# Sixteen instead of six weight chunks decoded during the first attention batch, later ones in three steps

## The chip, the cores and the metric

The kernel runs on one core of a Trainium2 chip. The metric is the device time of one execution in microseconds (us). The kernel before took 1181.28 to 1185.04 us in three runs, median 1183.97. One more execution was recorded by the profiler; everything read from a trace here comes from it.

## The reference

Attention with a threshold, then two feed-forward networks (FFN), one behind the other. The shapes are batch 4, 8 heads, 576 positions, head size 64; the FFNs see 2304 tokens of width 512 and have 2048 hidden units.

```python
scores = matmul(q, k.T) / sqrt(64)
scores = where(scores >= max(scores) - tau, scores, -1e9)
attn = softmax(scores)                       # over the last axis
x = matmul(attn, v)                          # heads side by side: 2304 x 512
h = x @ moe_w_in                             # first FFN: leaky, alpha per hidden unit
x = (max(h, 0) + alpha * min(h, 0)) @ moe_w_out
h = x @ moe2_w_in                            # second FFN
out = (h * clip(h + 3, 0, 6) / 6) @ moe2_w_out
```

Activations are float32, but the four weight matrices arrive as float64.

## The kernel before

**Attention** goes over 16 pairs of heads, 4 pairs for each of the 4 batches, and each pair has 9 tiles of queries: 144 tiles, 36 to a batch. A tile (`do_S`, `soft`) is a score matmul into PSUM, a row maximum and a threshold on VectorE, an exponential on ScalarE, and a masked sum on VectorE. Every second tile is followed by a division on GpSimd, transposes, and the product with v. Loads, splits and transposes for the next pair (`prep`) are emitted between the tiles of the present one.

**The FFNs** go over blocks of 512 tokens, one for each batch, and a block of the 256 left-over tokens. Each block passes through layer 1 and layer 2 with 16 hidden slices (`ft`). `h_group` makes one slice: 12 matmuls with the chunk `wi` of the input weights, an activation and a split of the result. `o_group` multiplies four slices with their chunks `wo` of the output weights. A list of such groups (`queue`) is worked off beside the attention of the following batches: block 0 runs beside the attention of batch 1, and so on. The last batch's block and the left-overs come behind the attention.

**Weights.** Each of the four matrices has 16 chunks, 64 in all, and is used once for each block. A value is used as two float32r parts, high and low: `split` copies the high part on ScalarE and subtracts it for the low part on VectorE or GpSimd (L102, L103). For its first use a chunk must also be decoded from float64 to float32. `decode_load` fetches 512 KB into one of three raw buffers (`raw64`). `decode` runs two instructions on ScalarE (L149, L150), three on VectorE (L151, L153, L154) and one on GpSimd (L155), and stores the 256 KB result to a scratch in device memory (L157). Its result `f` lies in the `stage` pool, which has four slots and also takes the loads from scratch (`st`, L170). Later blocks load the chunk from scratch and split it.

The first six chunks are decoded between the tiles of the first batch (`decode_early`, `EARLY = 6`); they are loaded back from scratch when block 0 comes to them. The other 58 are fetched by `fetch` and decoded and split by `ready`, both called from `h_group` of block 0, one group ahead of the use. The split parts lie in the pools `wip` (two chunks of `wi`) and `wop` (five chunks of `wo`).

**The order** on each engine is not that of the code. A scheduler takes the instructions of all engines by priority as soon as it expects their inputs and slots to be there; attention has its priority raised (`tc.high_priority`). On the chip each engine then works through its list in that fixed order, and all DMAs here are issued by SyncE (SP), in one list too.

Of the kernel before, what the change touches and what calls it, by code (L numbers as in the profile page):

```python
# [27 lines left out]
def f32(ap):  # L28
    return ap.bitcast(F32)
# [3 lines left out]
def kernel(  # L33
# [17 lines left out]
    NF = DFF // P  # L51
# [7 lines left out]
    NB = S // P  # L59
    W = S + SR  # L60

    EARLY = 6
    LAG = 3

    OG = 4
# [11 lines left out]
    def pool(stack, name, bufs, **kw):  # L77
        return stack.enter_context(tc.tile_pool(name=name, bufs=bufs, **kw))

    const = pool(ctx, "const", 1)  # L80
    stage = pool(ctx, "stage", 4)
    gp = pool(ctx, "gp", 5)
    tmp = pool(ctx, "tmp", 2)
    wip = pool(ctx, "wip", 2)
# [16 lines left out]
    def split(hi, lo, src, lo_eng):  # L101
        nc.scalar.copy(hi, src)  # L102
        lo_eng.tensor_tensor(out=lo, in0=src, in1=f32(hi), op=ALU.subtract)  # L103
# [3 lines left out]
    wide = moe_w_in.dtype != F32  # L107
# [7 lines left out]
    def chunk(nm, ft):  # L115
        w = weights[nm]
        if nm[0] == "i":
            n = w.shape[1] // NF
            return w[:, ft * n:(ft + 1) * n].rearrange("(k p) f -> p k f", p=P)
        return w[ft * P:(ft + 1) * P, :]  # L120
# [2 lines left out]

    RA, RB, RG = 27, 19, 20
    raw64 = []
    for i in range(3 if wide else 0):
        t = const.tile([P, RA * RB, 2], U32, name=f"raw64{i}")
        nc.gpsimd.memset(t[:, DM:], 0)
        raw64.append(t)

    def rows(ap):
        return ap.rearrange("p (a b) -> p a b", a=RA)[:, :, 0:RB]

    def st_tile(dt, name):
        return stage.tile([P, RA * RB], dt, tag="st", name=name)

    def decode_load(nm, ft):
        raw = raw64.pop(0)
        raw64.append(raw)
        dst = raw[:, 0:DM]  # L140
        dst = dst.rearrange("p (k f) a -> p k (f a)", k=NKT) if nm[0] == "i" else dst.rearrange("p n a -> p (n a)")
        nc.sync.dma_start(dst, chunk(nm, ft))
        return raw

    def decode(nm, ft, raw):
        f = st_tile(U32, "f")
        cl = dec.tile([P, RA * RG], U32, tag="cl", name="cl", bufs=2)
        low = dec.tile([P, RA * RG, 2], U16, tag="low", name="low", bufs=2)
        nc.scalar.activation(rows(low[:, :, 0]), rows(raw[:, :, 0]), AF.Copy, scale=2.0 ** -29)  # L149
        nc.scalar.activation(f32(f), f32(raw[:, :, 1]), AF.Abs)  # L150
        nc.vector.tensor_scalar(out=rows(low[:, :, 1]), in0=rows(raw.bitcast(U16)[:, :, 3]), scalar1=0x8000, scalar2=0x4000,  # L151
                                op0=ALU.bitwise_and, op1=ALU.bitwise_xor)
        nc.vector.tensor_scalar(out=rows(f32(cl)), in0=rows(f32(f)), scalar1=F64_HI, scalar2=F64_LO, op0=ALU.min, op1=ALU.max)  # L153
        nc.vector.tensor_single_scalar(rows(f), rows(cl), 3, op=ALU.logical_shift_left)  # L154
        nc.gpsimd.tensor_tensor(out=rows(f), in0=rows(f), in1=rows(low.bitcast(U32).rearrange("p n a -> p (n a)")), op=ALU.add)  # L155
        f = f32(f)[:, 0:DM]
        nc.sync.dma_start(scratch[nm, ft], f)  # L157
        return f

    raws = {}  # L160

    def w_fetch(key, nm, ft, fresh=False):
        if key in raws:
            return
        if wide and fresh:
            raws[key] = decode_load(nm, ft)
            return
        t = st_tile(F32, "st")[:, 0:DM]
        if wide:
            nc.sync.dma_start(t, scratch[nm, ft])  # L170
        elif nm[0] == "i":
            nc.sync.dma_start(t.rearrange("p (k f) -> p k f", k=NKT), chunk(nm, ft))
        else:
            nc.sync.dma_start(t, chunk(nm, ft))
        raws[key] = t
# [3 lines left out]
    passes = [(layer, b) for b in list(range(B - 1)) + [None] for layer in (1, 2)]  # L179
    decoded = set()  # L180
    ws = {}

    def w_of(kind, c):
        layer, blk = passes[c // NF]
        nm, ft = f"{kind}{layer}", c % NF
        return nm, ft, layer, blk, blk == 0 and (nm, ft) not in decoded

    def fetch(kind, c):
        if c < len(passes) * NF and (kind, c) not in ws:
            nm, ft, _, _, fresh = w_of(kind, c)  # L190
            w_fetch((kind, c), nm, ft, fresh)

    def ready(kind, c):
        if c < len(passes) * NF and (kind, c) not in ws:
            fetch(kind, c)
            nm, ft, layer, blk, fresh = w_of(kind, c)
            t = raws.pop((kind, c))
            if wide and fresh:
                t = decode(nm, ft, t)
            w = (wip if kind == "i" else wop).tile([P, 2, DM], F32R, tag="w" + kind, name="w" + kind)  # L200
            if fresh:
                on_dve = layer == 2 and ft % 4 == 3
            else:
                on_dve = ft % 4 < (1 if layer == 1 and blk is not None else 2)
            split(w[:, 0], w[:, 1], t, nc.vector if on_dve else nc.gpsimd)
            ws[kind, c] = w
# [31 lines left out]
    def g_hi(g, n):  # L238
        gs = gp.tile([P, 2, SM], F32R, tag="gs", name="gs")
        nc.scalar.copy(gs[:, 0, :n], g[:, :n])  # L240
        return gs
# [223 lines left out]
    def x_ready(blk):  # L465
        if ("x", 1, blk) not in box:
            box["x", 1, blk] = x0 if blk == 0 else load_x(new_x(), x1d[blk], blocks[blk], nc.gpsimd)

    def ffn_groups(layer, blk):
        n = blocks[blk]  # L470
        c0 = passes.index((layer, blk)) * NF
        gs = {}
        accs = []

        def h_group(ft):
            c = c0 + ft
            ready("i", c)
            if ft == 0 and layer == 1:
                x_ready(blk)
            fetch("i", c + 1)  # L480
            fetch("o", c)
            h = ps_ho.tile([P, SM], F32, tag="ho", name="h")
            mm_h(h, ws["i", c], box["x", layer, blk], n)
            g = act1(h, ft, n) if layer == 1 else act2(h, ft, n)
            gs[ft] = g_hi(g, n)
            g_lo(gs[ft], g, n)
            ready("i", c + 1)
            ready("o", c)
            if ft == NF - 1 and layer == 2 and blk + 1 in emitted and blk + 1 < B - 1:
                x_ready(blk + 1)  # L490

        def o_group(qt, dt):
            last = qt == NF // OG - 1
            if qt == 0 and dt == 0:
                accs.append(xp.tile([P, ND, SM], F32, tag="acc", name="acc"))
            if last and dt == 0 and layer == 1:
                box["x", 2, blk] = new_x()
            o = ps_ho.tile([P, SM], F32, tag="ho", name="o")
            for f in range(OG):
                ft = OG * qt + f  # L500
                (mm_o1 if layer == 1 else mm_o2)(o, ws["o", c0 + ft], gs[ft], dt, n, f == 0, f == OG - 1)
            a = accs[0][:, dt, :]
            if qt == 0:
                nc.scalar.activation(a, o, AF.Copy, scale=1.0 if layer == 1 else 1.0 / 6.0)
            elif layer == 1:
                nc.vector.tensor_tensor(out=a, in0=o, in1=a, op=ALU.add)  # L506
            else:
                nc.vector.scalar_tensor_tensor(out=a, in0=o, scalar=1.0 / 6.0, in1=a, op0=ALU.mult, op1=ALU.add)
            if last and layer == 1:
                y = box["x", 2, blk]  # L510
                split(y[:, 0, dt], y[:, 1, dt], a, nc.vector)
            elif last:
                store(blk, dt, a)

        seq = [(h_group, (ft,)) for ft in range(OG)]
        for qt in range(NF // OG):
            nxt = [(h_group, (ft,)) for ft in range(OG * qt + OG, min(NF, OG * qt + 2 * OG))]
            for d in range(ND):
                seq.append((o_group, (qt, d)))
                if d != 2:  # L520
                    seq += nxt[:1]
                    nxt = nxt[1:]
            seq += nxt
        return seq

    def new_x():
        return xp.tile([P, 2, NKT, SM], F32R, tag="x", name="x")
# [10 lines left out]

    early_dec = [(nm, ft) for ft in range(NF) for nm in ("i1", "o1")][:EARLY]

# [32 lines left out]
    for i in range(NS):  # L573
# [10 lines left out]
        if i % PB == PB - 1:  # L584
            emitted.add(i // PB)
        if wide and i % 2 == 1 and i < 2 * EARLY + 3:
            decode_early(i // 2)
# [20 lines left out]
    for layer in (1, 2):  # L608
# [6 lines left out]
        for m in range(len(seq) + LAGO):  # L615
            if m < len(seq):
                ft, blk = seq[m]
# [12 lines left out]
            ft, blk = seq[m - LAGO]  # L630
# [5 lines left out]
            if layer == 1:  # L636
                for d in range(ND):
                    o = oa[d][:, 0:n] if blk < B else orr[d // 2][:, (d % 2) * 256:(d % 2) * 256 + n]
# [3 lines left out]
            else:  # L642
                for d in range((n + P - 1) // P):
                    o = oa[d] if blk < B else orr[d]
# [41 lines left out]
```

## Time and profile before

| | |
|---|---|
| median of 3 runs | 1183.97 us |
| profiled execution, its own time | 1181.22 us |
| its span, first to last instruction | 1179.4 us |
| TensorE busy (matmul) | 1127.3 us, 96% |
| VectorE, ScalarE, GpSimd busy | 650.5, 663.2, 672.9 us (55 to 57%) |
| granted TensorE clock, mean | 0.994 |
| DMA | 139.09 MB, mean 118 GB/s |

PE is TensorE, PEld its weight loads, DVE VectorE, ACT ScalarE, POOL GpSimd, SP SyncE. Busy shares are means over stretches that differ: attention alone up to about 136 us, then FFN and attention together, then FFN alone. A busy TensorE is one with a matmul under way, which need not be at its best rate. In a table by stretch, the cells are PE, PEld, DVE, ACT and POOL in this order, each busy microseconds with the number of instructions, then PEclk (the granted clock as a share of 2.4 GHz), the busy share of the 16 DMA engines and GB/s.

### The profile page before, as it was taken

How to read it: one execution, taken by the hardware profiler on the slowest of the kernel's cores; microseconds unless marked ns; L12 is line 12 of the kernel's file. 1: busy time of each engine (PE TensorE's matmuls, PEld its weight loads, DVE VectorE, ACT ScalarE, POOL GpSimd, SP SyncE). 2: the span in 40 equal slices, each digit the busy share in tenths (PEclk: the TensorE clock that was granted, in tenths of full speed). 3: DMA queues.
4: the chain of work that ended last, by engine and by line, in shares of the span. 5: the costliest groups of instructions: out<-in, count | busy, mean ns of one | idle time of the engine just before them, and what ended most of it. 6: DMA issues, size and time to landing. Idle time of an engine off the chain costs nothing.

```text
span 1179.4 us, 19483 instructions
## 1 busy us (share of the span) xinstructions
PE 1127.3 (96%) x6944; PEld 933.8 (79%) x6944; DVE 650.5 (55%) x1297; ACT 663.2 (56%) x1272; POOL 672.9 (57%) x713
## 2 busy tenths in 40 slices
PE   6789999999999999999999999999999999999998
PEld 5568787777777878888887878887778888888886
DVE  6877798979697554556363637373226333331221
ACT  6778688678787645456655555455534222243332
POOL 2765589887889665555454755545334434334432
PEclk9899999999999999999999999999999999999999
DMA  6843256475766534242424432322234322222211
GB/s 173 257 132 85 72 181 214 150 235 192 241 199 183 159 102 119 72 124 78 118 68 119 141 99 73 101 75 72 82 90 154 89 63 63 63 63 64 63 36 54
DMA packets 93634, 139.09 MB, mean 118 GB/s; under 512 B 19424, under 2 KB 48608, under 8 KB 93536
## 3 DMA queue, kind: packets, MB, share of 16 engines
q1 hardware_dynamic: 93536, 137.83, 39.4%
q8 instruction: 55, 0.90, 0.3%
q14 instruction: 43, 0.35, 0.1%
HBM read 103.29 MB, written 25.17 MB: 109 GB/s over the span
## 4 chain that ended last, share of the span: by engine, by line
PE 63%; DVE 5%; ACT 4%; issue 3%; DMA 2%; POOL 2%; DVEq 0%; ACTq 0%; POOLq 0%; SPq 0%
PE h L218 25%; PE o L254 14%; PE o L248 11%; PE s L380 3%; PE pv L444 3%; PE t L426 2%; PE r L248 2%; PE r L254 2%; DMA st<-wo 1%; DMA raw<-in_moe_w_out_dram 1%; DVE nmx L401 1%; DVE g L226 1%; ACT m L232 1%; POOL wo L103 1%; DVE m L223 1%
## 5 line engine op out<-in xcount | busy, mean ns | idle before, releaser
L218 PE MATMUL h<-x,wi 128*128 128x512 f32 (+1 forms) x1536 | 354.6, 380 | 0.8 <-DVE acc L506 0.6
L218 PEld LDWEIGHTS h<-x,wi 128*128 128x128 f32 x1536 | 272.8, 188 | 53.0 <-DVE acc L506 1.0
L244 POOL TENSOR_TENSOR gs<-g,gs 128x512 fp32r<-128x512 f32 (+1 forms) x160 | 191.4, 1196 | 212.7 <-ACT gs L240 211.9
L254 PE MATMUL o<-wo,gs 128*128 128x512 f32 x768 | 195.2, 399 | 7.0 <-DVE g L234 4.3
L248 PE MATMUL o<-gs,wo 128*128 128x512 f32 x768 | 193.8, 398 | 6.0 <-DVE acc L506 2.2
L254 PEld LDWEIGHTS o<-wo,gs 128*128 128x128 f32 x768 | 141.1, 189 | 39.9 <-DVE g L234 6.7
L248 PEld LDWEIGHTS o<-gs,wo 128*128 128x128 f32 x768 | 140.0, 188 | 38.3 <-DVE g L226 4.7
L234 DVE SCALAR_TENSOR_TENSOR g<-m,h 128x512 f32<-128x512 f32 x80 | 50.5, 632 | 164.3 <-ACT m L232 163.1
L223 DVE TENSOR_SCALAR m<-h,alpha_sb 128x512 f32<-128x512 f32 x80 | 55.6, 695 | 148.1 <-PE h L218 147.9
L402 ACT ACTIVATE e<-s,nmx 128x576 f32<-128x576 f32 x144 | 106.7, 745 | 40.8 <-DVE nmx L401 40.1
L240 ACT CAST gs<-g 128x512 fp32r<-128x512 f32 (+1 forms) x160 | 92.8, 580 | 61.8 <-DVE g L226 27.6
L404 DVE SCALAR_TENSOR_TENSOR e<-s,thr,e 128x576 f32<-128x576 f32 x144 | 116.1, 812 | 20.2 <-ACT e L402 17.9
L401 DVE TENSOR_REDUCE nmx<-s 128x1 f32<-128x576 f32 x144 | 107.6, 751 | 30.7 <-PE s L380 30.3
L413 POOL TENSOR_SCALAR e<-e,rc 128x576 f32<-128x576 f32 x144 | 109.3, 770 | 25.6 <-DVE rc L410 23.8
L103 POOL TENSOR_TENSOR wi<-st,wi 128x512 fp32r<-128x512 f32 x58 | 75.0, 1294 | 80.2 <-ACT wi L102 80.0
L232 ACT ACTIVATE m<-h,three 128x512 f32<-128x512 f32 x80 | 51.5, 645 | 114.7 <-PE h L218 111.9
L444 PE MATMUL pv<-p,v 128*64 128x128 f32 (+1 forms) x1600 | 108.9, 271 | 5.3 <-DVE g L234 2.0
L102 ACT CAST wo<-st 128x512 fp32r<-128x512 f32 x99 | 59.0, 619 | 96.0 <-DMA st<-wo 83.8
L444 PEld LDWEIGHTS pv<-p,v 128*64 128x64 f32 x1600 | 83.6, 138 | 29.0 <-issue 16.6
L103 POOL TENSOR_TENSOR wo<-st,wo 128x512 fp32r<-128x512 f32 x58 | 76.9, 1341 | 52.1 <-ACT wo L102 52.0
L380 PE MATMUL s<-ka,qt 128*128 128x288 f32 x512 | 100.7, 323 | 5.0 <-DVE thr L403 3.1
L102 ACT CAST wi<-st 128x512 fp32r<-128x512 f32 x99 | 60.9, 615 | 79.0 <-PE h L218 41.8
(86 smaller groups left out, 1603.9 us busy)
## 6 DMA issues: line engine op xcount, KB each, us to landing
st<-wi SPq DMA_DIRECT2D x99, 256.0 KB, 2.7
st<-wo SPq DMA_DIRECT2D x99, 256.0 KB, 2.7
raw<-in_moe_w_in_dram SPq DMA_DIRECT2D x32, 512.0 KB, 4.8
raw<-in_moe_w_out_dram SPq DMA_DIRECT2D x32, 512.0 KB, 4.2
ka<-ka SPq DMA_DIRECT2D x30, 304.0 KB, 4.5
wi<-f SPq DMA_DIRECT2D x32, 256.0 KB, 3.2
wo<-f SPq DMA_DIRECT2D x32, 256.0 KB, 4.1
raw<-in_k_dram SPq DMA_DIRECT2D x16, 256.0 KB, 3.4
```

The lines of the kernel that those rows point to most:

```text
L102: nc.scalar.copy(hi, src)
L103: lo_eng.tensor_tensor(out=lo, in0=src, in1=f32(hi), op=ALU.subtract)
L218: nc.tensor.matmul(h[:, :n], lhsT=w[:, ws, kt * P:(kt + 1) * P], rhs=x[:, xs, kt, :n], start=(i == 0), stop=(i == len(steps) - 1))
L244: nc.gpsimd.tensor_tensor(out=gs[:, 1, :n], in0=g[:, :n], in1=f32(gs[:, 0, :n]), op=ALU.subtract)
L248: nc.tensor.matmul(o[:, :n], lhsT=w[:, ws, dt * P:(dt + 1) * P], rhs=gs[:, gsel, :n], start=fresh and start and i == 0, stop=stop and i == ...
L254: nc.tensor.matmul(o[:m, :], lhsT=gs[:, gsel, tt * P:tt * P + m], rhs=w[:, ws, :], start=start and i == 0, stop=stop and i == 2)
L380: nc.tensor.matmul(ps[:, half, 0:SH], lhsT=w, rhs=s["k"][:, a, c + half * SH:c + half * SH + SH], start=(n == 0), stop=(n == len(mms) - 1))
L401: nc.vector.tensor_reduce(out=nmx, in_=ps, axis=AX.XY, op=ALU.max, negate=True)
L402: nc.scalar.activation(eh, ps, AF.Exp, bias=nmx, scale=1.0)
L404: nc.vector.scalar_tensor_tensor(out=eh, in0=ps, scalar=thr, in1=eh, op0=ALU.is_ge, op1=ALU.mult, accum_out=sm[:, h:h + 1])
L413: nc.gpsimd.tensor_scalar(out=eh, in0=eh, scalar1=rc[:, h:h + 1], scalar2=0.0, op0=ALU.mult, op1=ALU.add)
L444: nc.tensor.matmul(pv[64 * h:64 * h + 64, :], lhsT=vn[:, h, kt, :], rhs=pt[:, blk, c:c + m], start=(kt == 0), stop=(kt == NB), skip_group_ ...
```

## The change

Sixteen chunks instead of six are in the list that is decoded in the first batch. The `stage` pool has six slots instead of four, and there are four raw buffers instead of three. A new function `ahead` is called twice in `h_group`: with step 0 it fetches the raw chunk `wi` three groups and `wo` two groups ahead of its use, with step 1 it decodes the chunk two groups and one group ahead. `ready` then only splits what is decoded already.

```diff
-    EARLY = 6
+    EARLY = 16
...
-    stage = pool(ctx, "stage", 4)
+    stage = pool(ctx, "stage", 6)
...
-    for i in range(3 if wide else 0):
+    for i in range(4 if wide else 0):
...
+    inflight = set()
+
+    def ahead(kind, c, step):
+        if not wide or c >= len(passes) * NF or (kind, c) in ws:
+            return
+        nm, ft, _, _, fresh = w_of(kind, c)
+        if not fresh:
+            return
+        if step == 0:
+            w_fetch((kind, c), nm, ft, True)
+        elif (kind, c) in raws and (kind, c) not in inflight:
+            raws[kind, c] = decode(nm, ft, raws[kind, c])
+            inflight.add((kind, c))
+
     def ready(kind, c):
...
-            if wide and fresh:
+            if wide and fresh and (kind, c) not in inflight:
                 t = decode(nm, ft, t)
...
             fetch("i", c + 1)
             fetch("o", c)
+            ahead("i", c + 3, 0)
+            ahead("o", c + 2, 0)
...
             ready("i", c + 1)
             ready("o", c)
+            ahead("i", c + 2, 1)
+            ahead("o", c + 1, 1)
```

The order on the engines moves with it. The first place is VectorE's list in the first batch, around the eighth and ninth attention tile. `nmx` is the row maximum that begins a tile, `e` its masked sum; `low`, `cl` and `f` are the three steps of a decode. Before:

```order
L401 TENSOR_REDUCE nmx_541<-s_536 128x1
L154 TENSOR_SCALAR f_656<-cl_657 128x513
L153 TENSOR_SCALAR cl_741<-f_740 128x27x19
L151 TENSOR_SCALAR low_742<-raw641_166 128x27x19
L403 TENSOR_SCALAR thr_542<-nmx_541,ntau_sb_210 128x1
L401 TENSOR_REDUCE nmx_603<-s_592 128x1
L154 TENSOR_SCALAR f_740<-cl_741 128x513
L153 TENSOR_SCALAR cl_831<-f_830 128x27x19
L404 SCALAR_TENSOR_TENSOR e_528,sm_529<-s_536,thr_542,e_528 128x576
L403 TENSOR_SCALAR thr_604<-nmx_603,ntau_sb_210 128x1
```

Of the change:

```order
L417 TENSOR_REDUCE nmx_543<-s_538 128x1
L420 SCALAR_TENSOR_TENSOR e_530,sm_531<-s_525,thr_533,e_530 128x576
L153 TENSOR_SCALAR cl_743<-f_742 128x27x19
L153 TENSOR_SCALAR cl_833<-f_832 128x27x19
L151 TENSOR_SCALAR low_744<-raw640_164 128x27x19
L419 TENSOR_SCALAR thr_544<-nmx_543,ntau_sb_212 128x1
L154 TENSOR_SCALAR f_742<-cl_743 128x513
L154 TENSOR_SCALAR f_832<-cl_833 128x513
L151 TENSOR_SCALAR low_834<-raw641_166 128x27x19
L420 SCALAR_TENSOR_TENSOR e_530,sm_531<-s_538,thr_544,e_530 128x576
L417 TENSOR_REDUCE nmx_605<-s_594 128x1
```

About one decode stood between two tiles; now there are two. Counted over the list, ten decodes stand before tile 18 before the change and sixteen with it, the last of them at tile 13.

The second place is the same list where the FFN of block 0 begins. `m` and `g` are the activation of one hidden slice. Before:

```order
L226 SCALAR_TENSOR_TENSOR g_1850<-h_1835,m_1848 128x512
L401 TENSOR_REDUCE nmx_2266<-s_2255 128x1
L403 TENSOR_SCALAR thr_2267<-nmx_2266,ntau_sb_210 128x1
L153 TENSOR_SCALAR cl_2098<-f_2097 128x27x19
L404 SCALAR_TENSOR_TENSOR e_2264,sm_2265<-s_2255,thr_2267,e_2264 128x576
L154 TENSOR_SCALAR f_2097<-cl_2098 128x513
L223 TENSOR_SCALAR m_1878<-h_1865,alpha_sb_94 128x512
L410 RECIPROCAL rc_2273<-den_2272 128x1
L226 SCALAR_TENSOR_TENSOR g_1880<-h_1865,m_1878 128x512
```

Of the change:

```order
L242 SCALAR_TENSOR_TENSOR g_1962<-h_1947,m_1960 128x512
L417 TENSOR_REDUCE nmx_2316<-s_2305 128x1
L419 TENSOR_SCALAR thr_2317<-nmx_2316,ntau_sb_212 128x1
L420 SCALAR_TENSOR_TENSOR e_2314,sm_2315<-s_2305,thr_2317,e_2314 128x576
L239 TENSOR_SCALAR m_1990<-h_1977,alpha_sb_94 128x512
L426 RECIPROCAL rc_2323<-den_2322 128x1
L242 SCALAR_TENSOR_TENSOR g_1992<-h_1977,m_1990 128x512
```

Between the first two activations the steps of a decode are gone. Between attention tiles 44 and 49 five decodes stand before, one with the change; between tiles 50 and 80 it is 49 and 47.

## Rows read from the trace of the kernel before

**Rows 1.** The page's busy times, share of the span and instructions.
```profile
PE 1127.3 (96%) x6944; PEld 933.8 (79%) x6944; DVE 650.5 (55%) x1297; ACT 663.2 (56%) x1272; POOL 672.9 (57%) x713
```

**Rows 2.** Stretches: start:end, length, busy us per engine, PEclk, DMA share, GB/s.
```profile
21.40:73.20 51.80, 41.32 (x294) 31.10 (x292) 42.36 (x92) 41.12 (x82) 33.09 (x39) 0.90 0.80 246
73.20:136.00 62.80, 59.71 (x561) 48.12 (x560) 44.56 (x117) 49.92 (x108) 35.63 (x59) 1.00 0.26 69
136.00:416.00 280.00, 265.46 (x1656) 217.66 (x1655) 230.97 (x448) 213.74 (x398) 231.68 (x236) 0.99 0.62 191
141.00:173.20 32.20, 32.07 (x209) 26.99 (x207) 29.12 (x60) 27.12 (x52) 28.03 (x32) 1.00 0.51 157
416.00:543.00 127.00, 125.48 (x789) 104.34 (x789) 69.94 (x144) 65.65 (x130) 72.14 (x78) 1.00 0.35 97
```

**Rows 3.** Stretches, the row maxima (L401, one a tile) alone on VectorE.
```profile
21.40:73.20 51.80, 9.72 (x13) 0.90 0.80 246
73.20:136.00 62.80, 19.12 (x26) 1.00 0.26 69
```

**Rows 4.** Stretch, the last decode step on VectorE (L154) alone.
```profile
21.40:73.20 51.80, 6.71 (x10) 0.90 0.80 246
```

**Rows 5.** VectorE in order of time from 261 us: start, us, instruction.
```profile
261.25 0.68 DVE L154 TENSOR_SCALAR f<-cl 128x513 uint32<-128x513 uint32 x1
261.85 0.68 DVE L226 SCALAR_TENSOR_TENSOR g<-h,m 128x512 f32<-128x512 f32 x1
262.45 0.67 DVE L153 TENSOR_SCALAR cl<-f 128x513 f32<-128x513 f32 x1
263.04 0.77 DVE L151 TENSOR_SCALAR low<-raw 128x513 uint16<-128x513 uint16 x1
263.70 0.20 DVE L403 TENSOR_SCALAR thr<-nmx,ntau_sb 128x1 f32<-128x1 f32 x1
```

**Rows 6.** Groups of instructions: count, busy us, mean ns, idle before and releasers.
```profile
L149 ACT ACTIVATE low<-raw 128x513 uint16<-128x513 uint32 x64 | 52.8, 835 | 7.6 <-POOL f L155 6.3 <-DMA raw<-in_moe_w_in_dram 1.0 <-DMA raw<-in_moe_w_out_dram 0.3
L150 ACT ACTIVATE f<-raw 128x513 f32<-128x513 f32 x64 | 43.5, 682 | 20.0 <-POOL wi L103 4.0 <-DMA wo<-f 3.9 <-POOL wo L103 3.3
```

**Rows 7.** DMA from 21.4 to 73.2: totals; issues, KB, median us to landing.
```profile
DMA packets 8433, 12.77 MB, mean 246 GB/s; under 512 B 1355, under 2 KB 5488, under 8 KB 8427
...
raw<-in_moe_w_out_dram SPq DMA_DIRECT2D x5, 512.0 KB, 4.0
...
wi<-f SPq DMA_DIRECT2D x6, 256.0 KB, 2.5
...
raw<-in_k_dram SPq DMA_DIRECT2D x2, 256.0 KB, 5.4
```

**Rows 8.** Stretches of 5 us inside the early one.
```profile
35.00:40.00 5.00, 1.56 (x7) 0.84 (x7) 3.23 (x8) 2.10 (x6) 2.63 (x4) 0.85 0.99 319
40.00:45.00 5.00, 5.00 (x30) 4.38 (x29) 3.39 (x8) 3.78 (x8) 2.78 (x3) 0.50 0.89 268
```

**Rows 9.** ScalarE's waits, 21.4 to 73.2: total us, times, longest.
```profile
ACT f L150 <- DMA raw<-in_moe_w_out_dram: 2.8, 1, 2.8
ACT f L150 <- DMA wo<-f: 2.8, 1, 2.8
```

**Rows 10.** TensorE's waits, 136 to 416 us, the largest.
```profile
PE o L248 <- DVE acc L506: 2.2, 2, 1.2
```

**Rows 11.** ScalarE's waits, 136 to 416 us.
```profile
ACT f L150 <- POOL wi L103: 4.0, 5, 1.5
...
ACT f L150 <- POOL wo L103: 3.3, 5, 1.1
```

**Rows 12.** VectorE's waits, 136 to 416 us, the largest.
```profile
DVE cl L153 <- ACT f L150: 10.6, 9, 2.2
```

**Rows 13.** DMA issues of the whole kernel, the page.
```profile
raw<-in_k_dram SPq DMA_DIRECT2D x16, 256.0 KB, 3.4
```

**Rows 14.** The matmuls of h by line: duration ns, first and last start us.
```profile
L218 PE MATMUL h<-x,wi x1536: 277/389/615, 136.0 to 1033.6; 128*128 128x512 f32 x176, 128*128 128x256 f32 x16
```

## The prediction, made before the changed kernel ran

> **What bounds the kernel now.** I read the busy table first: TensorE is busy 96% of the span [rows 1], so time can only come from stretches where it is not. The table by stretch shows where those are [rows 2]. In the passes after the first batch it is idle 127.0 - 125.5 = 1.5 us in 127. From 136 to 416 us, the FFN of block 0 with the second batch's attention beside it, it is idle 280 - 265.5 = 14.5 us. From 21.4 to 73.2 us, early in the first batch, it is idle 51.8 - 41.3 = 10.5 us and works at a granted clock of 0.90. These two are the stretches in which weight chunks are decoded: 10 of the 64 in the first [rows 4], the other 54 in the second.
>
> I call 21.4 to 73.2 us the early stretch. It holds 13 attention tiles; the next 62.8 us hold 26 [rows 3], 2.42 us each, with no decode. At that pace 13 tiles would take 31.4 us; they take 51.8. Ten decodes and the six weight splits among them therefore cost 20.4 us, 2.0 us a decode. No single engine is full there: VectorE 42.4 of 51.8, ScalarE 41.1, GpSimd 33.1, and the DMA engines carry 0.80 of their time [rows 2]. Four resources pass each decode along, each with its own queue, and each is near its end.
>
> **What the change really moves.** The words say six early chunks become sixteen. In the emitted order that is less. Before, the scheduler already ran ten decodes by the attention tile 17; now all sixteen stand by tile 13, mostly two to a tile. So six decodes move, not ten. The FFN loses five before it reaches tile 50 in VectorE's queue (five there before, one now, with one DVE split more); from tile 50 to 80 there are 49 before and 47 now. The last one stands at tile 80 in both.
>
> **The early stretch, +9 us.** One decode on VectorE is three instructions. Start to start in a full queue they take 0.60 (L154), 0.59 (L153) and 0.66 us (L151), together 1.85 [rows 5]; six more are 11.1 us. ScalarE gets 6 x (0.835 + 0.682) = 9.1 us [rows 6]; GpSimd has 18.7 us free for its one instruction a decode. On the DMA queue a decode is one 512 KB load and one 256 KB store [rows 7], 0.79 MB, six are 4.7 MB on top of the 12.8 MB now moved there.
>
> From below: if every gap closes, VectorE needs 42.4 + 11.1 = 53.5 us, 1.7 more than now; ScalarE needs 50.2 and fits. At the 319 GB/s that the DMA engines reach at a 0.99 share [rows 8], 17.5 MB take 54.8 us, 3.0 more. So the floor is +2 to +3, not zero. From above: six decodes at the present 2.0 us are +12; VectorE at its present share (42.4 / 51.8 = 0.82) would need 65.3 us, +13.5. Two stalls inside the present price need not come back. ScalarE waited once 2.8 us for a raw load, once 2.8 us for the store of an earlier decode, whose staging slot it needed [rows 9]; a fourth raw buffer and six staging slots are there for both. Without the 5.6 us a decode costs (20.4 - 5.6) / 10 = 1.5 us, and six cost 8.9. That lies nearest to how the stretch behaves now, and I take +9, bounds +2 and +13.5.
>
> Nothing covers this: the first FFN matmul stands behind attention tile 43 in TensorE's order in both kernels, so whatever the first batch loses is lost to everything after.
>
> TensorE's clock: after TensorE had been busy 1.56 of 5 us, it ran the next 5 us at 0.50, the 1.2 GHz level [rows 8]. Over the stretch 0.90 means 10.4 us at that level, about as long as TensorE idles there. The sum takes 0 for more of it, because VectorE and the DMA set the pace there and TensorE catches up. In the Trainium skill, TensorE: Matmul & The Clock Gate, section What's actually happening, the slow clock is the default and activity releases it. By that rule nine more idle microseconds would bring about nine more at 1.2 GHz, worth 4.5 us of matmul, and the forecast would be 1194.5 instead; the row of the idle 5 us and the slow 5 us behind it agrees with the direction, and the row on VectorE's load speaks against the price.
>
> The DMA's floor also has a page: DMA: Bandwidth & Descriptors in the Trainium skill, section Specifications, gives about 358 GB/s as a core's share of its memory. By it, as an estimate, 17.5 MB take 48.9 us and the DMA would add nothing; the 319 GB/s of the trace is at a share of 0.99, so the measurement decides.
>
> **Reloads.** Ten more chunks come back from scratch (16 instead of 6), 256 KB each: 2.6 MB. Of these, seven are issued in the first batch behind its decodes, in the 62.8 us whose DMA share is 0.26 [rows 2]; I take 0, and 1.8 MB / 0.319 = 5.8 us of DMA time if that cover were gone. The last three wait for a staging slot until the FFN frees one, and on the SP queue the q load of a later pair stands behind them. It is needed six attention tiles later, at 2.42 us at least 14 us; cost 0, and if the wait were longer, what it exceeds that by. The split count does not change; one memset more is nothing.
>
> **The FFN of block 0, -3 us.** What can come back: 14.5 us of idle TensorE less what the later passes show anyway, 280 / 127 x 1.5 = 3.3, so 11.2 us at most. The five decodes that leave first stand around 141 to 173 us, where TensorE is busy 32.07 of 32.2 us: nothing to gain there [rows 2]. Where TensorE does wait, it waits for activations and accumulators from a full VectorE, 2.2 us the largest item, not for weights [rows 10], and that part of the queue loses 2 decodes of 49, by share 0.04 x 11.2 = 0.5 us. The staging slots are worth more. ScalarE stood 7.3 us before its decode step for splits that had to free a slot, and VectorE 10.6 us for ScalarE's step [rows 11, 12]. Six slots should remove most of the first; TensorE feels a part, as it is idle 14.5 us while VectorE is idle 280 - 231 = 49. I take 7.3 x 14.5 / 49 = 2.2, with the 0.5 about -3. Bounds: 0, or +2 for an order that happens to fall worse, and -11.
>
> The wide fetch distance itself I cost at 0: TensorE's list has no wait for a weight split, so a chunk that is ready a group earlier is only ready.
>
> **The sum.** The profiled execution took 1181.22 us, span 1179.4 and 1.8 around it. 1181.2 + 9 - 3 = 1187.2. The median of the runs shown, 1183.97, lies 2.8 above the profiled one, so the forecast for a median is 1190.
>
> **Rivals.**
> First, the gaps swallow it. The six decodes fall into VectorE's 9.4 and ScalarE's 10.7 idle microseconds, at the floor of +2 to +3, and the FFN gives 3 back: 1184, no change. For it: more buffers let the queues run full. Against: a decode costs 2.0 us now with the same gaps on offer. 0.2.
>
> Second, faster. In the FFN the slot waits are what starts the stalls: decode held up, VectorE late, activation late, TensorE idle. With six slots and loads issued two or three groups ahead, TensorE's idle falls to the rate of the later passes, -11, against +3 to +4 in the first batch: 1176. It decides where the FFN returns more than the early stretch takes. For it: 7.3 and 10.6 us of such waits. Against: VectorE is busy 231 of 280 us there and its order from tile 50 to 80 is nearly the same. 0.15.
>
> Third, much slower: the early stretch stays at its present 246 GB/s, and two decodes to a tile simply queue: 17.5 / 0.246 = 71 us, +19, less 3: 1200. For it: a k load took 5.4 us there against 3.4 over the kernel [rows 7, 13]. Against: the two stalls of 2.8 us kept the rate down. 0.15. The Trainium skill, DMA: Bandwidth & Descriptors, section Queues, rings and completion order, says each DMA engine consumes its descriptors in ring order, so an attention load issued behind four raw loads would wait for them; the 5.4 us agree.
>
> **How the numbers follow.** The forecast, 1190, has 0.5; its own range is 1185 to 1196. Faster or slower by 0.3% is 3.6 us, about what a measurement of this kernel can tell from no change. Slower: most of the forecast's 0.5, say 0.45, and the third rival's 0.15: 0.6. Same: most of the first rival, 0.17, and 0.05 from the forecast: 0.22. Faster: the second rival, 0.15, and 0.03 from the first: 0.18. The range leaves out the second rival's far end and the third's: from 1180 to 1198.
>
> **What would show it.** The first FFN matmul at about 145 us instead of 136 [rows 14], and the sixteen decodes closing by about 70 us at an attention pace of 5.5 to 6 us a tile. VectorE's busy share in that stretch above 0.85. From there on, TensorE's idle time over block 0's FFN between 9 and 14 us. ScalarE's wait for the store gone. Wrong if the first FFN matmul still starts before 140, or if the 280 us of block 0 shrink by more than 8.

## The result and the profile after

The changed kernel takes 1193.65 us (median of 4 runs, 1192.72 to 1194.56), the kernel before 1183.12 (4 runs beside it and earlier, 1181.28 to 1185.04). The ratio is 1.0089, 95% interval 1.007 to 1.0108: slower by 0.9%, 10.5 us by the medians. The forecast was 1190.

The two profiled executions lie further apart, 1181.22 and 1194.56 us, spans 1179.4 and 1192.8. The one of before is about the fastest of its runs, the one of after the slowest. Where the 13.4 us of the spans went is clean to read, since the kernel falls into three pieces at two instructions: the first and the 385th matmul of `h`, which begin and end block 0's FFN.

| | before | after | difference |
|---|---|---|---|
| first batch, to the first FFN matmul | 136.0 us | 151.2 | +15.2 |
| FFN of block 0, both layers | 279.9 | 279.0 | -0.9 |
| the rest | 763.5 | 762.6 | -0.9 |

The whole loss is in the first batch. In the busy times by stretch (columns as in [rows 2]), 62.3 and 87.1 us are the starts of the score matmuls of the attention tiles 13 and 18 in the kernel after, where the kernel before was at 55.0 and 73.2. First its two rows, then those of the kernel after:

```profile
21.40:55.00 33.60, 26.52 (x188) 19.66 (x186) 27.89 (x59) 27.03 (x54) 20.01 (x25) 0.90 0.82 258
55.00:73.20 18.20, 14.79 (x108) 11.45 (x107) 14.47 (x34) 14.09 (x30) 13.08 (x14) 0.91 0.74 225
```

```profile
21.40:62.30 40.90, 29.65 (x191) 23.56 (x190) 37.11 (x75) 33.37 (x64) 25.16 (x31) 0.75 0.93 295
62.30:87.10 24.80, 16.71 (x105) 13.39 (x104) 17.01 (x39) 16.49 (x31) 13.70 (x17) 0.73 0.90 291
21.40:87.10 65.70, 46.36 (x294) 36.95 (x292) 54.12 (x113) 49.85 (x95) 38.86 (x47) 0.74 0.92 294
87.10:151.20 64.10, 61.33 (x563) 48.91 (x561) 43.77 (x114) 49.67 (x107) 36.64 (x58) 1.00 0.29 77
151.20:430.10 278.90, 265.90 (x1655) 217.60 (x1654) 218.75 (x431) 207.41 (x386) 222.11 (x229) 0.99 0.58 177
430.10:556.80 126.70, 125.95 (x791) 104.73 (x790) 72.96 (x143) 66.31 (x131) 73.75 (x77) 1.00 0.35 98
```

The early stretch, again 13 tiles, has grown from 51.8 to 65.7 us [rows 2]. Up to tile 13 VectorE is 0.91 busy (37.11 of 40.9), behind it only 0.69. The DMA engines are at 0.92 of their time throughout, and TensorE's granted clock has fallen from 0.90 to 0.74; the same 294 matmuls were busy 46.4 us instead of 41.3 [rows 2]. The row maxima and the last decode step alone, as in [rows 3, 4], say that it is the same 13 tiles with 16 decodes instead of 10:

```profile
21.40:87.10 65.70, 9.78 (x13) 0.74 0.92 294
...
21.40:87.10 65.70, 10.66 (x16) 0.74 0.92 294
```

In the DMA of that stretch, against [rows 7], there are 6.5 MB more. Ten of the sixteen reloads are among them, issued from 64 to 85 us; before there were six. The k loads land after 6.2 us instead of 5.4:

```profile
DMA packets 12538, 19.29 MB, mean 294 GB/s; under 512 B 1630, under 2 KB 7832, under 8 KB 12531
...
st<-wi SPq DMA_DIRECT2D x6, 256.0 KB, 3.5
...
st<-wo SPq DMA_DIRECT2D x4, 256.0 KB, 4.1
raw<-in_k_dram SPq DMA_DIRECT2D x2, 256.0 KB, 6.2
```

ScalarE's waits up to tile 13, and then from tile 13 to 18 (total us, times, longest), are to be set against [rows 9]:

```profile
ACT f L150 <- DMA raw<-in_moe_w_out_dram: 4.7, 2, 3.4
...
ACT f L150 <- DMA raw<-in_moe_w_in_dram: 1.1, 2, 0.6
...
ACT wo L102 <- DMA st<-wo: 3.7, 1, 3.7
...
ACT wi L102 <- DMA st<-wi: 1.4, 2, 1.2
```

The wait for a staging slot is gone. In its place ScalarE waits 5.8 us for raw loads, and then for reloads from scratch. The longest of these, in ScalarE's list in order of time (the last bracket is the idle time before, and who ended it), and under it the row maximum on VectorE that the exponential `e` needs:

```profile
76.74 0.59 ACT L443 COPY p<-t 128x512 f32<-128x512 f32 x1 [0.51 <-PE t L442]
80.98 0.62 ACT L102 CAST wo<-st 128x512 fp32r<-128x512 f32 x1 [3.65 <-DMA st<-wo]
81.50 0.73 ACT L418 ACTIVATE e<-s,nmx 128x576 f32<-128x576 f32 x1
```

```profile
77.70 0.76 DVE L417 TENSOR_REDUCE nmx<-s 128x1 f32<-128x576 f32 x1 [0.53 <-PE s L396]
```

A split of a `wo` chunk, whose first `o` matmul comes at 170.8 us, 90 us later, stands in front of an attention tile's exponential. ScalarE is idle for 3.65 us. The row maximum was there at 78.46 us, so the exponential, at 81.50, starts 3.0 us later than its input allowed.

### The profile page after: what moved, and what is told of

It reads as the page before. It is cut to its first block, busy times and chain, and to the rows that moved or that the text cites. A ratio compares the mean times of both kernels' runs of the same rounds, so it can differ in the third digit from the quotient of the medians.

```text
span 1192.8 us, 19498 instructions
## 1 busy us (share of the span) xinstructions
PE 1134.6 (95%) x6944; PEld 940.9 (79%) x6944; DVE 663.4 (56%) x1299; ACT 665.2 (56%) x1272; POOL 678.7 (57%) x712
## 4 chain that ended last, share of the span: by engine, by line
PE 66%; ACT 4%; DVE 2%; issue 1%; POOL 0%; DVEq 0%; ACTq 0%
PE h L234 27%; PE o L270 14%; PE o L264 11%; PE pv L460 3%; PE s L396 3%; PE t L442 2%; PE r L264 2%; PE r L270 2%; ACT m L248 1%; PE pt L341 1%; DVE g L250 1%; ACT wi L102 1%; DVE acc L528 0%; PE r L445 0%; ACT e L418 0%
## 5 line engine op out<-in xcount | busy, mean ns | idle before, releaser
L103 POOL TENSOR_TENSOR wi<-st,wi 128x512 fp32r<-128x512 f32 x62 | 80.6, 1300 | 93.4 <-ACT wi L102 91.2
L418 ACT ACTIVATE e<-s,nmx 128x576 f32<-128x576 f32 x144 | 106.6, 746 | 34.1 <-DVE nmx L417 33.1
L460 PE MATMUL pv<-p,v 128*64 128x128 f32 (+1 forms) x1600 | 111.3, 275 | 6.7 <-ACT p L443 3.7
L102 ACT CAST wi<-st 128x512 fp32r<-128x512 f32 x104 | 64.0, 616 | 94.8 <-PE h L234 57.8
L442 PE MATMUL t<-ident,e 128*128 128x128 f32 x576 | 92.3, 288 | 12.0 <-POOL e L429 9.4
L103 POOL TENSOR_TENSOR wo<-st,wo 128x512 fp32r<-128x512 f32 x62 | 86.9, 1420 | 12.1 <-ACT wo L102 11.9
```

Of the source, the lines that this page charges most:

```text
L418: nc.scalar.activation(eh, ps, AF.Exp, bias=nmx, scale=1.0)
L442: nc.tensor.transpose(ps[:, kt], e[:, c:c + P], ident)
L460: nc.tensor.matmul(pv[64 * h:64 * h + 64, :], lhsT=vn[:, h, kt, :], rhs=pt[:, blk, c:c + m], start=(kt == 0), stop=(kt == NB), skip_group_ ...
```

## Experiments

Theory and rivals for the 15 us: the DMA engines at 0.92; VectorE, with 11.8 us more work in a list that was already crowded; TensorE's clock at 0.74; the reloads. For what could be won: the larger pools, the fetch ahead, and where in the first batch a decode stands. In all runs the third piece took 762.3 to 763.5 us, so two numbers tell of each: the start of the first FFN matmul and the length of block 0's FFN, from the profiled execution. They are of one execution each, and the times of one kernel differ by 2 to 8 us from run to run, so a difference of 2 us in one of them says little. Ratios are against the kernel before on the same chip, with 95% intervals.

| run | decodes before the FFN | first FFN matmul | block 0's FFN | median | ratio |
|---|---|---|---|---|---|
| before | 10 | 136.0 | 279.9 | 1183.12 | |
| after | 16 | 151.2 | 279.0 | 1193.65 | 1.0089 (1.007 to 1.0108) |
| e1_early6 | 13 | 142.3 | 276.7 | 1180.88 | 0.9979 (0.9968 to 0.9989) |
| e2_only_early16 | 16 | 148.5 | 280.8 | 1193.91 | 1.0093 (1.0071 to 1.0114) |
| e3_dma_alone | 0 whole | 129.5 | 277.1 | 1171.43 | 0.9901 (0.9885 to 0.9917) |
| e4_half_load | 16 | 149.5 | 277.1 | 1189.64 | 1.0055 (1.0034 to 1.0075) |
| e5_spread | 12 | 137.4 | 274.8 | 1176.64 | 0.9944 (0.9927 to 0.9961) |
| e6_score_twice | 16 | 155.3 | 278.2 | 1197.79 | 1.0114 (1.0099 to 1.013) |
| e7_no_clamp | 16 | 136.0 | 277.4 | 1176.10 | 0.9931 (0.9914 to 0.9947) |
| e8_few_spread | 8 | 128.9 | 283.1 | 1175.02 | 0.9918 (0.9896 to 0.994) |
| e9_pools_alone | 13 | 140.4 | 274.4 | 1178.61 | 0.9962 (0.9945 to 0.9979) |
| e10_reloads_held | 16 | 146.1 | 284.5 | 1193.63 | 1.0081 (1.0057 to 1.0106) |
| e11_before_spread | 8 | 128.9 | 284.8 | 1180.18 | 0.9976 (0.9961 to 0.9991) |
| e12_ten_spread | 10 | 134.3 | 279.6 | 1180.83 | 0.9973 (0.9958 to 0.9987) |

**Which resource makes the early stretch long.** First all but one instruction of an early decode goes, and the DMA stays:

```diff
...
+        if light:
+            nc.scalar.activation(f32(f), f32(raw[:, :, 1]), AF.Abs)
+            f = f32(f)[:, 0:DM]
+            nc.sync.dma_start(scratch[nm, ft], f)
+            return f
...
-            decode(nm, ft, raws.pop((nm, ft)))
+            decode(nm, ft, raws.pop((nm, ft)), light=True)
```

> The change with the decode of the 16 early chunks cut to its one instruction on ScalarE that fills f (left out: the other five instructions, on ScalarE, VectorE and GpSimd); loads, stores and reloads stay whole. Theory DMA: the 19.3 MB of the early stretch at about 294 GB/s set it, so the first FFN matmul stays at 147 to 151 us and the time at 1189 to 1193. Rival, the engines: 16 x 1.85 us less on VectorE lets the tiles run at their pace without decode, first FFN matmul at 130 to 136 us, time 1175 to 1181.

The other way round, half the raw load goes, and the instructions stay (the raw buffers are zeroed whole at the start, so that the other half holds something):

```diff
...
+        if half:
+            dst, src = (dst[:, 0:2], src[:, 0:2]) if nm[0] == "i" else (dst[:, 0:DM], src[:, 0:DM])
```

> The change with only half of each of the 16 early raw chunks loaded (256 KB instead of 512 KB each, 4.2 MB less in all; the other half of a chunk is left out); all decode instructions stay. Theory DMA: (19.3 - 4.2) / 0.294 = 51.4 us instead of 65.7, first FFN matmul at about 138 us, time about 1181. Rival, the engines: VectorE has the same 54 us of work in the stretch; first FFN matmul stays at 148 to 151, time 1190 or more.

The 13 tiles of e3_dma_alone, and under them those of e4_half_load, up to tile 13, from there to tile 18, and together:

```profile
21.40:59.30 37.90, 34.23 (x292) 27.93 (x291) 22.43 (x58) 32.61 (x69) 16.66 (x28) 0.95 0.95 318
```

```profile
21.40:65.20 43.80, 32.42 (x222) 24.16 (x220) 40.06 (x82) 36.79 (x71) 26.34 (x33) 0.81 0.64 199
65.20:85.60 20.40, 17.06 (x96) 12.85 (x95) 14.13 (x30) 14.20 (x27) 11.54 (x15) 0.67 0.95 304
21.40:85.60 64.20, 49.47 (x317) 37.02 (x315) 54.20 (x111) 50.99 (x98) 37.88 (x47) 0.76 0.74 232
```

The theory DMA falls for these 13 tiles. With the DMA engines at 0.95 and 318 GB/s the 13 tiles take 37.9 us, and the first FFN matmul comes 21.7 us earlier than in the changed kernel. With the DMA share down to 0.74 they take 64.2, nearly as long as 65.7, and the first FFN matmul comes 1.7 us earlier. VectorE's work, 54.2 us, is that of the changed kernel. The share falls to 0.64 up to tile 13, where the time, 43.8 us, is no shorter than 40.9; from tile 13 to 18 it is still 0.95, so there this run tests less. Waits for the DMA are there in the changed kernel, as shown, but its full share is not what sets the pace. Behind tile 18 the run doesn't clear the DMA: from there to the first FFN matmul e3 takes 70.2 us, 6.1 more than the changed kernel, and why is not shown.

**VectorE by itself.** One of its three instructions is left out of the early decodes:

```diff
...
-        nc.vector.tensor_scalar(out=rows(f32(cl)), in0=rows(f32(f)), scalar1=F64_HI, ...
+        if clamp:
+            nc.vector.tensor_scalar(out=rows(f32(cl)), in0=rows(f32(f)), scalar1=F64_HI, ...
-        nc.vector.tensor_single_scalar(rows(f), rows(cl), 3, ...
+        nc.vector.tensor_single_scalar(rows(f), rows(cl if clamp else f), 3, ...
```

> The change with the clamp (cl, one of three VectorE instructions of a decode) left out for the 16 early chunks, 16 x 0.59 = 9.4 us less on VectorE; DMA, ScalarE and GpSimd unchanged. Theory VectorE: it is 0.91 busy from tile 5 to 13, so the first FFN matmul comes 7 to 10 us earlier, at 141 to 144, time about 1185. Rival, the chain through all queues or the DMA: it comes less than 4 us earlier, time 1190 or more.

The 13 tiles of e7_no_clamp, up to tile 13, from there to tile 18, and together:

```profile
21.40:54.40 33.00, 25.81 (x187) 18.48 (x185) 27.39 (x58) 28.48 (x57) 19.89 (x25) 0.90 0.91 290
54.40:71.10 16.70, 13.71 (x109) 10.34 (x109) 15.59 (x34) 16.03 (x34) 14.85 (x17) 1.00 1.01 316
21.40:71.10 49.70, 39.52 (x295) 28.82 (x293) 42.97 (x91) 44.51 (x90) 34.74 (x41) 0.93 0.94 299
```

9.4 us less on VectorE take 15.2 us off the first batch, with the DMA as full as in the changed kernel (0.94, 299 GB/s). More comes back than was taken away, and the halves say why. With shorter decodes the scheduler also put them less tightly, up to tile 17 instead of 13. Up to tile 13, where VectorE was 0.91 busy, it has 9.7 us less to do and the tiles take 7.9 us less. The time there follows VectorE's work, nearly one for one, and ScalarE's waits for raw loads fall with it, from 5.8 to 1.3 us. From tile 13 to 18 it has only 1.4 us less to do, but the tiles take 8.1 us less. There ScalarE has no split of a reload at all (the first is at 72.6 us), where the changed kernel has five with 5.1 us of waits. So the run took away two causes, and only the first half speaks for VectorE. Whether it binds there as a full engine or as a link of the chain from ScalarE over VectorE to GpSimd, the run doesn't separate: the missing instruction shortens both.

**The clock.** The score matmuls of the tiles 5 to 19 are issued twice. These are 68 matmuls more, at the full clock 0.13 us each from start to start in this run's trace, 9 us:

```diff
-        for half in range(2):
+        for half in range(2) if not 5 <= i < 20 else (0, 1, 0, 1):
```

> The change with the score matmuls of attention tiles 5 to 19 issued twice, which keeps TensorE at work in the early stretch (the second writes the same scores). Theory clock: the 0.74 granted there (0.90 before the change) is what makes the stretch long; with more work the clock comes to 0.85 or more and the first FFN matmul to 140 to 147 us in spite of 8 us more matmul. Rival, the engines' queues: the stretch is no shorter, first FFN matmul at 151 to 158 us, time 1193 to 1201.

The stretch up to 90 us in e6_score_twice:

```profile
21.40:90.00 68.60, 51.70 (x360) 41.10 (x359) 53.48 (x110) 50.58 (x96) 40.40 (x50) 0.88 0.88 282
```

The clock rises to 0.88, and the first FFN matmul comes 4.1 us later. So the lower clock is mostly a mark of TensorE's waiting. That 9 us of matmul cost only 4.1 leaves room for a price of the clock of up to 5 us, as much as the 5.0 us by which the same matmuls were busy longer; this run can't separate it from matmuls that fill gaps.

**The reloads.** They are held back to the FFN's start by a small write that waits for a row maximum:

```diff
+        if wide and key[1] < EARLY // 2:
+            nc.gpsimd.tensor_scalar(out=t[:, 0:1], in0=st["nmx"], scalar1=1.0, scalar2=0.0, op0=ALU.mult, op1=ALU.add)
...
+        st["nmx"] = nmx
```

> The change with the reloads of the 16 early chunks held back until the tiles in which the FFN of block 0 starts, by a write of one element a row that waits for a row maximum; the decodes stand as in the change. If the reloads in front of the first batch's attention on ScalarE and on the DMA queue (waits of 3.7 and 1.4 us) are what makes tiles 13 to 18 take 24.8 us, these fall to 15 to 18 us, the first FFN matmul comes at 142 to 146 and the time is about 1187. Rival: the backlog of the burst itself (decodes and their stores) is the cause, the first FFN matmul stays at 149 or later, time 1191 or more; the reloads, now bunched at the FFN's start, can only add.

The same two halves of the stretch in e10_reloads_held:

```profile
21.40:62.40 41.00, 28.88 (x191) 22.96 (x190) 36.98 (x75) 33.07 (x64) 24.97 (x31) 0.74 0.94 296
62.40:82.20 19.80, 15.76 (x105) 12.65 (x104) 15.95 (x37) 14.27 (x26) 11.15 (x15) 0.77 0.77 236
```

Both cases are partly right. Up to tile 13 nothing changes, 41.0 us; tiles 13 to 18 fall from 24.8 to 19.8, and the first FFN matmul comes 5.1 us earlier. But the reloads are now issued from 140 to 173 us, around the FFN's start, block 0's FFN grows by 5.5 us, and the time is the same (medians 1193.63 and 1193.65). So the reloads do cost 5 us where they stand, and the move gave nothing. That the reloads at their new place are what lengthens the FFN is likely, but not shown by itself.

**The parts of the change.** Back to a list of six, and the list of sixteen alone (each is the number of `EARLY`), and the two pool sizes alone:

> The change with the early list back at 6 chunks; six staging slots, four raw buffers and the three-step fetch stay. In its order 13 decodes stand before attention tile 20 (10 before the change, 16 with it). If the price lies in the number of decodes in the first batch (15.2 us for six in the changed kernel, 2.5 each), three more cost 7 to 8 us: first FFN matmul at about 143.5 us, time about 1190. If the larger pools and the fetch ahead pay for themselves in the FFN of block 0, that stretch (280 us before, 279 changed) falls to 270 or less and the time is about 1182.

> The kernel before with the early list at 16 chunks and nothing else. All 16 decodes stand by attention tile 15. If the loss is the longer list alone, the first FFN matmul comes at 148 to 153 us and the time is 1193 to 1199, as much as the whole change or a little more, since the FFN of block 0 gets no larger pools. If the larger pools are what lets the decodes crowd into tiles 5 to 13 and so make them dear, it is 142 or earlier and the time at most 1189.

> The kernel before with six staging slots and four raw buffers and nothing else (early list 6, no fetch ahead). Its order is nearly that of e1_early6: 13 decodes before attention tile 18. If the fetch and decode a group earlier does nothing, as the prediction had it, the time is that of e1_early6, 1179 to 1183, with block 0's FFN at 276 to 278 us. If the fetch ahead is what shortened that FFN in e1 (276.7 us against 279.9), it stays at 279 to 281 here and the time is 1184 to 1187.

The longer list alone costs all of it (1.0093). Without it the rest of the change is a small gain (0.9979), and the pools alone have that gain too (0.9962). A gain from fetching and decoding a group earlier isn't to be seen: with the pools alone block 0's FFN is 274.4 us, with the fetch ahead 276.7. The first FFN matmul comes later in both, since with free slots the scheduler pulls 13 decodes ahead of the FFN instead of 10; so their shorter FFN also has three decodes fewer. In e1 the expected 1190 was missed: the start was as forecast for that case (142.3), but the FFN gave more back, and the profiled run, 1183.8, was the slowest of ten.

**Spreading.** A raw load waits for the row maximum of an attention tile, so decodes can't crowd:

```diff
-    EARLY = 16
+    EARLY = 12
+    GAP = 3
...
+            nc.gpsimd.tensor_scalar(out=f32(raw64[0][:, 0:1, 0]), in0=gate, scalar1=1.0, scalar2=0.0, op0=ALU.mult, op1=ALU.add)
             w_fetch((nm, ft), nm, ft, True)
...
-        if wide and i % 2 == 1 and i < 2 * EARLY + 3:
-            decode_early(i // 2)
+        if wide and i % GAP == 1 and i < GAP * EARLY + 3:
+            decode_early(i // GAP, st["nmx"])
```

> The change with 12 early chunks whose raw loads are held back, one for every three attention tiles, by a write of one element a row that waits for that tile's row maximum; 13 decodes then stand between tiles 5 and 44 instead of 5 and 13. If the price of a decode comes from the burst (DMA at 0.92 of its time, two decodes to a tile), the spread ones fall into the stretch where the DMA share is 0.26 and cost 1 us or less: first FFN matmul at 125 to 132 us, time 1173 to 1180, faster than both. If a decode costs 2 to 2.5 us of the first batch wherever it stands, first FFN matmul at about 143, time about 1189.

> Like e5_spread, with 8 early chunks, one for every four attention tiles, and the first ten later raw loads held back in the same way until the tiles in which the FFN starts: 8 decodes before tile 32, then none before tile 41. A spread decode cost 1.4 us of the first batch in e5 (pairs of 27.5 and 25.7 us against 23.4 and 21.2 before, with three decodes each); in the FFN of block 0 it costs 10 / 54 = 0.2 us by the excess idle of before. If that holds, the first FFN matmul comes at 129 to 133 us, the FFN stretch stays below 278, time 1169 to 1174. Rival: VectorE, 231 of 280 us busy there, is the next bound, the FFN stretch takes 281 or more and the time is 1176 to 1180, no better than e5.

e8 has `EARLY = 8`, `GAP = 4`, and the same write before the first ten later loads. Its stretches, the first 13 tiles, from there to the FFN, block 0's FFN:

```profile
21.60:60.20 38.60, 35.23 (x296) 27.81 (x294) 29.52 (x70) 30.28 (x64) 21.86 (x36) 0.96 0.48 134
60.20:128.90 68.70, 61.11 (x560) 49.13 (x558) 53.00 (x131) 57.00 (x120) 46.05 (x73) 0.98 0.54 153
128.90:412.00 283.10, 269.07 (x1656) 218.97 (x1655) 231.87 (x456) 217.84 (x404) 235.28 (x243) 0.99 0.64 197
```

Both beat both kernels, e8 by 0.8% against before. They have shorter lists too, 12 and 8 chunks; no run spreads all sixteen. In e8 the 13 tiles take 38.6 us, nearly as fast as in e3, which runs only one instruction of each decode; only four of the eight decodes end among these tiles. In e5 the first FFN matmul, at 137.4 us, lies between its two cases. In e8 the first FFN matmul came where it was expected, but block 0's FFN took 283.1 us instead of less than 278: the decodes taken out of the first batch cost time in the FFN after all, and e8 lies between its two forecasts.

> The kernel before with the spreading of e8_few_spread alone: 8 early chunks, one for every four tiles, the first ten later loads held; four staging slots, three raw buffers, no fetch ahead. If spreading is the whole gain of e8, the time is 1174 to 1178. If the larger pools carry a part of it in the FFN of block 0, it is 1178 to 1182.

> Between e5 and e8: the change with 10 early chunks, one for every three tiles, and the first four later loads held. A decode costs 1.4 us in the first batch when spread, and the FFN of block 0 took 274.7 us in e5 (13 decodes ahead of it) and 283.1 in e8 (8). If the two trade one for one, this lies at 1174 to 1178 like both. If e8's longer FFN came from the ten held loads bunching at its start, this has the FFN at 275 to 278, the first FFN matmul at 130 to 133 and a time of 1170 to 1174.

Spreading on the kernel before, with eight chunks in the list instead of six, is worth 0.2% (0.9976); the time, 1180.18, is inside what the second case expected. The rest of e8's gain comes only with the larger pools and the fetch ahead beside it. Ten chunks (e12) met neither of its cases: first FFN matmul 134.3 and FFN 279.6, time 1180.83. That it is slower than e8 is outside both intervals; why, these runs don't show, and no model of one price a decode fits all the spread runs.

## Why the prediction was right, and where its sizes were off

**The direction and the reading of the order.** Right: six decodes moved, not ten; TensorE had nothing to gain where they left; the first batch's loss was passed on whole to all that followed, as the constant third piece shows. The time lies inside the range and inside the forecast's own range of 1185 to 1196. The sizes were less good than that looks: the terms make +6 us, and the medians differ by 10.5, the profiled executions by 13.4. The early stretch was taken 6.2 us too small and the FFN's return 2.1 too large, both to the same side. That 1190 is only 3.7 off the median is partly luck: it holds the 2.8 us between the profiled execution before and the median, while after the change the median lies 0.9 below the profiled one.

**The early stretch, +9.** Too small: +13.9 at tile 18, above its upper bound of 13.5, and +15.2 at the FFN. VectorE's share over the 13 tiles stayed at 0.82 (54.1 of 65.7), as that bound supposed, and not above 0.85, as the signs at the prediction's end had it; but it is a mean of 0.91 and 0.69. Of the other signs, the decodes did close by about 70 us, and the first FFN matmul, named for about 145 us, came at 151.2. Up to tile 13 the eight tiles took 40.9 us, 5.1 each, against 33.6: +7.3. The pace of 5.5 to 6 us a tile that was named there does not fit the prediction's own +9, which makes 60.8 us for 13 tiles, 4.7 each. GpSimd, called near its end too, was busy 33.1 of 51.8 us. The larger part of the miss lies behind tile 13. The prediction took out the two stalls of 2.8 us [rows 9] because larger pools were there for them. The store's stall did go, but ScalarE waited 5.8 us for raw loads instead, and tiles 13 to 18 grew from 18.2 to 24.8 us, though only three decodes end among them on VectorE, four before.

**Reloads, 0.** This is the term that was mis-sized. Seven of the ten additional ones were to come behind the decodes, where the DMA share was 0.26 [rows 2]. But ten of the sixteen were issued before tile 18, at a share of about 0.9, and the scheduler put five of their splits into ScalarE's list there, in front of exponentials; there were five before too, but these waited 1.6 us in all and now 5.1; an open DMA queue doesn't cover an instruction that waits for it in line. e10_reloads_held puts 5.1 us on it in the first batch. With 9 + 5 the first batch would have been +14.

**Bounds by VectorE and by the DMA.** The prediction kept both and leaned on neither. e3 and e4 say that the DMA does not bind the 13 tiles, e7 that VectorE's work does up to tile 13. The floor by the DMA happened to be close to the one by VectorE, so the sum did not suffer.

**The clock, 0.** In the Trainium skill, TensorE: Matmul & The Clock Gate, section What's actually happening, the slow clock is the default and activity releases it. The trace agrees with the direction: the granted clock fell from 0.90 to 0.74. TensorE was idle 8.9 us more in the stretch (19.3 instead of 10.5), close to the nine supposed. But a mean of 0.74 over 65.7 us means 34 us at the 1.2 GHz level against 10.4 before, so 24 more and not nine. The price worked out in the prediction, 4.5 us, is close to the 5.0 us by which the same matmuls were busy longer; whether the stretch paid it is neither shown nor excluded by e6, which leaves up to 5.

**The FFN of block 0, -3.** With the larger pools and the short list it gave 3.2 us in e1 and 5.5 in e9, with three decodes fewer in it. In the changed kernel it gave 0.9, and a wait had come in the place of the one removed. ScalarE's wait for a staging slot fell from 7.3 to 5.2 us [rows 11], but the wait for one of the two `low` buffers, which the pools left alone, rose. Before, and then after:

```profile
ACT low L149 <- POOL f L155: 5.8, 4, 3.3
```

```profile
ACT low L149 <- POOL f L155: 12.2, 11, 1.8
...
ACT f L150 <- POOL wo L103: 3.0, 5, 1.5
...
ACT f L150 <- POOL wi L103: 2.2, 1, 2.2
```

In e1 and e9 that wait for `low` is 6.7 and 3.6 us. That its rise is what took the gain away fits these numbers, but no run tests it.

TensorE's idle time there, 278.9 - 265.9 = 13.0 us, is within the 9 to 14 that were named as a mark.

**The rivals.** The gaps didn't swallow it. The faster one is refuted here, but its mechanism is the small gain of e1 and e9. The much slower one was named for the DMA: the rate did not stay at 246 GB/s, it rose to 294, and by e3 and e4 the DMA did not set the 13 tiles' pace.

## What to carry to other kernels

When work is moved to a place that has slack on average, look at when the scheduler will run it: a loop that hands out a piece every second tile does not hold the pieces apart. Here they crowd into the first few tiles, sixteen by tile 15 even with the old pools (e2), 13 instead of 10 with larger ones (e9). A cheap write that makes a load wait for a row of the work beside it spreads them. With shorter lists, 12, 10 and 8 chunks, the spread kernels gained 0.6, 0.3 and 0.8% where the change lost 0.9%; of this the short list and the pools have 0.2 to 0.4% without spreading (e1, e9). A transfer that is hidden costs nothing only if the instruction that takes it in is not in line before something that is needed now.

## What the runs showed of the hardware

The DMA engines can run at a share of 0.95 and 318 GB/s while attention tiles keep a pace of 2.9 us (37.9 us for 13 in e3_dma_alone); a full DMA share was no sign of a bound there. The granted clock of TensorE in the early stretch followed how long TensorE waited, from 0.74 in the changed kernel (46.4 of 65.7 us busy) to 0.95 in e3 (34.2 of 37.9), with nearly the same matmuls.
